# Placing a kernel's matmul operands modulo 256 bytes and gathering its second product's matmuls into one run

## The chip, the cores and the metric

The kernel runs on one core of a Trainium2 chip. The metric is the device time of one execution in microseconds, median of three runs; it was 1442.73 us before the change (1442.69 to 1444.27). The engines are called as the profile calls them: PE (TensorE's matmuls), PEld (its weight loads), DVE (VectorE), ACT (ScalarE), POOL (GpSimd), SP (SyncE).

## What is computed

Three layers in a row, all in float32: a banded attention, a gated feed-forward layer, and a mixture of eight experts whose gate is normalised over rows and columns eight times.

```python
attn_out = _attn_ref(q, k, v, ...)                 # 2 x 8 heads, 768 tokens, 64 wide
x = attn_out.transpose(0, 2, 1, 3).reshape(1536, 512)
h = x @ w_in                                       # 512 -> 2048
x = (h * sigmoid(h)) @ w_out                       # 2048 -> 512
P = exp(x @ w_gate - max)                          # 1536 x 8, then 8 rounds of row and column scaling
for e in range(8):
    h = maximum(x @ w1[e], 0)                      # 512 -> 1024
    out += P[:, e:e+1] * (h @ w2[e])               # 1024 -> 512
```

## The kernel before

**Numbers.** Every matmul operand is a pair of float32r tiles, a high part and the rest (`hi`, `lo`); a product is three matmuls: high by high, high by rest, rest by high. A matmul has a stationary operand, loaded ahead (PEld), and a streamed one.

**Stages.** Tokens go in three blocks of 512 (`TB`), numbered `tb` 0 to 2. Attention fills PE, DVE, ACT and POOL at the start and beside the first blocks of the feed-forward layer ("first layer" below). That layer has 48 steps of 128 hidden columns: 12 matmuls `h` (L237 to L239: stationary `w0`, streamed the tokens `x1`, high and rest) and 12 matmuls `y` (L276: stationary `w1`, streamed `hh`, `hl`). Four steps at the front are done in two halves of 256 tokens, the other 44 have 512 columns. The last block runs without attention beside it.

**Second layer** (`layer2`, from about 421 us). A unit `u` is one half of one expert's hidden columns and one token block: 8 x 2 x 3 = 48 units, `tb` fastest. Its first product, 512 tokens by 512 inputs by 512 hidden columns, is made by a seven-product scheme on 2 x 2 blocks. `x_combine` prepares seven combinations of the tokens in each block (`xc`, with four DVE sums and seven splits), `w_combine` seven combinations of the weights (`wc`, on POOL and ACT). Each of the seven products, numbered 0 to 6, is 12 matmuls of 256 streamed columns at L388 (`h_product`): stationary a slice of `wc[i]`, streamed a block of `xc[i]`. Four PSUM banks collect them: products 0 and 1 in the first (one buffer, tag `h`), 5 and 6 in the second, 4 and 2 in the third, 3 in the fourth (three buffers, tag `a`). DVE adds the banks (`u2` L476, `u3` L480, `h_sum` L410), ACT takes the positive part, DVE the rest (`h_split`, L402 and L403); the four hidden blocks go into five pairs of tiles, the rooms, in turn.

The second product of a unit, `y_part` (L423), is 48 matmuls of 512 streamed columns: four parts `k`, four token tiles `i`, three matmuls each; stationary a slice of a hidden block, streamed a row block of the second weights (`w2c`). `y_add` (L440) weights it by the gate and adds it to the output. It runs one window behind: window `u` computes the seven products of unit `u` and the second product of unit `u - 1`.

**Order in a window** (`window`, L445 to L497) is written by hand: products in `ORDER` 0, 5, 4, 6, 3, 1, 2, and `second()` puts one part of 12 second-product matmuls behind product 5, behind 4, behind 3 and behind 1. `side` is a generator with the rest of the gate (and the third block's `x_combine`); one step of it is taken behind each product. In the last token block of each weight set the next weights are combined product by product (`more`), and in the first block the second weights are split. A scheduler then places the instructions on each engine and moves a few where something would wait.

**Places.** Pools hand out places in a partition one tile behind another, and nearly all tiles are a multiple of 256 bytes long. So all of a pool starts at one byte address modulo 256, set by the odd sizes allocated ahead of it. In the built program these places are:

| operand | role | modulo 256 |
|---|---|---|
| `xc` of blocks 0 and 1 (pool late) | streamed, first product | 96 |
| `xc` of block 2 (pool x) | streamed, first product | 32 |
| `wc` of products 0, 5, 4 (`wc0` to `wc2`, late) | stationary, first product | 96 |
| `wc` of products 6, 3, 1, 2 (`wx0`, `wx1`, ring) | stationary, first product | 32 |
| hidden blocks `room_hh`, `room_hl`, `room_g` | stationary, second product | 32 |
| hidden block `roomh`, `rooml` (late) | stationary, second product | 96 |
| `w2c` (`wx0`, `wx1`, ring) | streamed, second product | 32 |
| first layer, all operands | both | 32 |

While a matmul streams its operand, the stationary operand of the next is loaded. So what stands beside each other in time is the streamed operand of one matmul and the stationary one of the next; by these places they are 0 apart for blocks 0 and 1 in products 0, 5 and 4, and for block 2 in products 6, 3, 1 and 2; streamed 64 above stationary for blocks 0 and 1 in products 6, 3, 1, 2; streamed 64 below (192 above) for block 2 in products 0, 5, 4, and for the second product where a hidden block lies in `roomh`, `rooml`.

Of the kernel before, what the change touches and what calls it, by code (L numbers as in the profile page):

```python
# [8 lines left out]
F32 = mybir.dt.float32  # L9
F32R = mybir.dt.float32r  # L10
# [5 lines left out]
ALU = mybir.AluOpType  # L16
# [4 lines left out]
P = 128  # L21
TB = 512
# [13 lines left out]
WF, RAW = 5, 3  # L36
RING = 4
HB = TB // 2
ORDER = 0, 5, 4, 6, 3, 1, 2
TINY = 1.125 * 2.0**-15  # L40


# [4 lines left out]
class Kernel:  # L47
# [29 lines left out]
    def setup(self, const, pre):  # L77
        nc = self.nc
        n16 = const.tile([P, 2, 4], U16, tag="n16", name="n16")
        for i, src in enumerate((self.n_global, self.n_local)):  # L80
            nc.sync.dma_start(
                n16[:, i, :], src.bitcast(U16).rearrange("(o f) -> o f", o=1).broadcast_to([P, 4])
            )
        self.att_load(0, pre)
        self.att_load(1, const)
        self.ident = const.tile([P, P], F32, tag="ident", name="ident")
        make_identity(nc, self.ident)
        rel, key = self.places(pre)
# [207 lines left out]

    def x_alloc(self, tb):

        if tb < self.NB - 1:
            tiles = [self.gp.tile([P, TB], F32R, tag=f"xc{tb}_{i}", name=f"xc{tb}_{i}") for i in range(14)]
        else:
            tiles = [x[:, c, :] for _ in range(2) for x in self.new_x(f"xc{tb}_{_}") for c in range(self.KD)]
        tiles = [t.rearrange("p (c w) -> p c w", c=2) for t in tiles]
        self.xc[tb] = tiles[:7], tiles[7:14]

    def x_combine(self, tb):
        v, x = self.nc.vector, self.x2[tb]
# [63 lines left out]
    def h_product(self, u, i):  # L373

        nc = self.nc
        ah, al = self.wc[i]
        bh, bl = (x[i] for x in self.xc[u % self.NB])
        name = {0: 0, 1: 0, 5: 1, 6: 1, 4: 2, 2: 2, 3: 3}[i]
        first = i in (0, 5, 4, 3)
        if first:  # L380
            self.hb[name] = self.bank("haaa"[name], f"h2_{u}_{i}")
        ps = self.hb[name]
        n = 0
        for f in range(2):
# [28 lines left out]
    def y_part(self, u, k, tiles=range(4)):  # L413

        nc = self.nc
        f = (2, 3, 0, 1)[k]
        wh, wl = self.w2c[f]
        for i in tiles:
            hh, hl = (x[:, f % 2, i % 2 * P:(i % 2 + 1) * P] for x in self.hq[u][f // 2, i // 2])
            if k == 0:  # L420
                self.y[i] = self.bank("y", f"y2_{u}_{i}")
            for j, (a, b) in enumerate(((hh, wh), (hh, wl), (hl, wh))):
                nc.tensor.matmul(  # L423
                    self.y[i], a, b, start=k == 0 and j == 0, stop=k == 3 and j == 2, skip_group_check=True
                )

    def y_add(self, u, i):

# [16 lines left out]

    def window(self, u, side):

        nc, n_units = self.nc, self.E * self.NH * self.NB
        q, tb = divmod(u, self.NB)
        y = iter(range(4)) if u else iter(())  # L450

        more = tb == self.NB - 1 and q + 1 < self.E * self.NH
        if more:
            self.w_load(q + 1, 1)

        def second():
            k = next(y, None)
            if k is not None:
                self.y_part(u - 1, k)
                if u % self.NB == 0:  # L460
                    self.w_split((2, 3, 0, 1)[k])

        def first(i):
            ps = self.h_product(u, i)
            if more:
                self.w_combine(i)
            next(side, None)
            return ps
# [12 lines left out]
        b4 = first(3)  # L481
        hq[1, 1] = self.h_sum(u3, b3, ALU.add)
        hq[1, 0] = self.h_sum(u3, b4, ALU.subtract)
        second()
        first(1)
        hq[0, 0] = self.h_split(b1)
        second()
        if u:
            if u > self.NB * self.NH:
                for _ in side:  # L490
                    pass
            for i in range(4):
                self.y_add(u - 1, i)
            del self.hq[u - 1]
        first(2)
        hq[0, 1] = self.h_sum(u2, b3, ALU.add)
        if tb == self.NB - 2 and q + 1 < self.E * self.NH:  # L497
            self.w_load(q + 1, 0)

    def layer2(self):  # L500
        n_units = self.E * self.NH * self.NB
        side = self.rest()
        for u in range(n_units):
            self.window(u, side)
        for i in range(4):
            for k in range(4):
                self.y_part(n_units - 1, k, (i,))
            self.y_add(n_units - 1, i)


# [42 lines left out]
    def gate_parts(self):  # L553
# [11 lines left out]
        for it in range(8):  # L565
# [226 lines left out]

    def new_x(self, name):

        return tuple(self.xp.tile([P, self.KD, TB], F32R, tag=t, name=f"{name}{t}", bufs=2) for t in ("xh", "xl"))

    def attention(self, sg):

# [110 lines left out]
    def finish(self):  # L909
# [2 lines left out]
        self.attending = False  # L912
        with tc.tile_pool(name="late", bufs=1, side="right") as self.gp:
            self.gate_load()
            extra = [
                tuple(self.gp.tile([P, TB], F32R, tag=f"wc{i}{t}", name=f"wc{i}{t}") for t in "hl") for i in range(3)
            ]
# [11 lines left out]
            for _ in parts:  # L929
                pass  # L930

            names = [(a, i) for i in range(RING) for a in (0, 1)]
            ws = extra + [
                tuple(self.ring.tile([P, self.DM], F32R, tag=f"w{a}{t}", name=f"wx{a}{t}_{i}") for t in "hl")
                for a, i in names
            ]
# [25 lines left out]
            yield from self.gate_logits(tb)  # L962

    def rest(self):

        yield from self.x_combine(self.NB - 1)
        yield
        yield from self.gate_logits(self.NB - 1)
        yield from self.gate_parts()
# [127 lines left out]
    def arm(self, path):  # L1097
        tc = self.tc
        self.slices, self.raws, self.wfs, self.hs, self.x1, self.x2, self.xc = {}, {}, {}, {}, {}, {}, {}
        with ExitStack() as ctx:  # L1100
# [2 lines left out]
            self.hp = pool(name="hid", bufs=1)  # L1103
            self.wf = pool(name="wf", bufs=WF)
            self.ring = pool(name="ring", bufs=RING)
            self.live = {"wf": 0, 0: 0, 1: 0}
            self.limit, self.stores = SPLIT_START, []
            self.nar, self.freed, self.next_load, self.next_nar, self.next_split = None, [], 0, 0, [0, 0]
# [41 lines left out]
```

## Time and profile before

| | |
|---|---|
| time, median of 3 runs | 1442.73 us (1442.69 to 1444.27) |
| the profiled execution: time, span | 1444.39 us, 1442.6 us |
| mean granted TensorE clock | 0.99 of full |
| PE busy | 1413.3 us, 98%, 8,552 matmuls |
| PEld busy | 1232.1 us, 85% |
| DVE, ACT, POOL busy | 739.9, 487.2, 553.6 us (51, 34, 38%) |
| moved by DMA | 92.18 MB, mean 64 GB/s |

The span is what the profile's records cover; the execution's own time, with what lies around it, is 1.8 us longer. Busy shares are means over stages that differ. A matmul's recorded duration (280 ns for 256 columns, 392 for 512) overlaps that of the next; how fast a run goes is read from the starts of its first and last matmul.

### The profile page before, as it was taken

What the parts mean: (1) busy time and instruction counts of PE and PEld (TensorE: products, weight loads), DVE (VectorE), ACT (ScalarE), POOL (GpSimd) and SP (SyncE); (2) the same over time, 40 slices, a digit from 0 to 9 for tenths busy, and PEclk for the clock granted to TensorE, in tenths of its full rate; (3) what the DMA queues carried; (4) which work ended last, traced back from release to release, by engine and by line L of the source; (5) the groups of instructions that cost most, each with busy time, mean ns of one, the idle gap of its engine ahead of it and who ended that gap; (6) DMA issues with size and microseconds to landing.
All of it is one profiled execution on the core that took longest, in us unless ns stands there. A gap on an engine that the chain in (4) does not pass through costs nothing.

```text
span 1442.6 us, 21250 instructions
## 1 busy us (share of the span) xinstructions
PE 1413.3 (98%) x8552; PEld 1232.1 (85%) x8552; DVE 739.9 (51%) x1298; ACT 487.2 (34%) x949; POOL 553.6 (38%) x489
## 2 busy tenths in 40 slices
PE   8998999999999999999999999999999999999998
PEld 6776687778888989999998999899899899989997
DVE  8899545456353556544354354435444443544443
ACT  6665545555352422222232221223222132322220
POOL 5677755444470423314142331414224141422210
PEclk8899999999999999999999999999999999999999
DMA  9685442222230201011010101102010110201001
GB/s 257 178 245 186 154 121 73 74 74 88 88 103 1 59 1 59 16 44 41 19 50 10 59 16 44 44 16 57 3 59 22 38 45 15 59 0 45 1 28 63
DMA packets 75292, 92.18 MB, mean 64 GB/s; under 512 B 30640, under 2 KB 49072, under 8 KB 75184
## 3 DMA queue, kind: packets, MB, share of 16 engines
q1 hardware_dynamic: 72880, 82.34, 19.2%
q10 hardware_dynamic: 2304, 8.39, 1.5%
q8 instruction: 69, 1.13, 0.3%
q14 instruction: 39, 0.32, 0.1%
HBM read 79.19 MB, written 11.53 MB: 63 GB/s over the span
## 4 chain that ended last, share of the span: by engine, by line
PE 89%; DVE 8%; issue 1%; ACT 1%; POOL 0%; DMA 0%; DVEq 0%; ACTq 0%; SPq 0%; POOLq 0%
PE y L423 37%; PE h L388 32%; PE y L276 7%; PE h L237 3%; PE h L238 3%; PE h L239 3%; PE a_s L726 2%; DVE wf L201 1%; DVE wf L203 1%; DVE wf L199 1%; DVE wf L205 1%; PE a_o L783 1%; PE a_f L764 1%; DVE s L735 1%; DVE st L744 0%
## 5 line engine op out<-in xcount | busy, mean ns | idle before, releaser
L480 DVE TENSOR_TENSOR tabs<-tabs,h 128x512 f32<-128x512 f32 x48 | 33.0, 687 | 333.9 <-PE h L388 333.9
L343 POOL TENSOR_TENSOR wc0l<-wf,wc0h 128x512 fp32r<-128x512 f32 x16 | 21.2, 1323 | 340.3 <-ACT wc0h L342 340.3
L440 DVE SCALAR_TENSOR_TENSOR x<-y,gate,x 128x512 f32<-128x512 f32 x168 | 115.5, 742 | 18.3 <-PE y L423 18.3
L343 POOL TENSOR_TENSOR wx1l<-wf,wx1h 128x512 fp32r<-128x512 f32 x64 | 89.9, 1405 | 79.7 <-ACT wx1h L342 79.5
L402 ACT ACTIVATE room_hh<-tabs 128x512 fp32r<-128x512 f32 x87 | 54.2, 629 | 190.9 <-DVE tabs L410 188.5
L410 DVE TENSOR_TENSOR tabs<-tabs,h 128x512 f32<-128x512 f32 x144 | 98.8, 687 | 19.0 <-PE h L388 16.8
L343 POOL TENSOR_TENSOR wx0l<-wf,wx0h 128x512 fp32r<-128x512 f32 x48 | 62.1, 1293 | 90.3 <-ACT wx0h L342 90.3
L388 PE MATMUL h<-xc,wx1h 128*128 128x256 f32 x512 | 93.4, 280 | 1.7 <-DVE tabs L410 1.7
L388 PE MATMUL h<-xc,wx0h 128*128 128x256 f32 x512 | 93.4, 280 | 0.6 <-DVE tabs L476 0.6
L423 PE MATMUL y<-wx1h,room_hh 128*128 128x512 f32 x232 | 91.2, 393 | 0.0
L423 PE MATMUL y<-wx0h,room_hh 128*128 128x512 f32 x232 | 91.2, 393 | 0.0
L423 PE MATMUL y<-wx0l,room_hh 128*128 128x512 f32 x232 | 90.8, 391 | 0.0
L423 PE MATMUL y<-wx1l,room_hh 128*128 128x512 f32 x232 | 90.8, 391 | 0.0
L423 PE MATMUL y<-wx0h,room_hl 128*128 128x512 f32 x232 | 90.7, 391 | 0.0
L423 PE MATMUL y<-wx1h,room_hl 128*128 128x512 f32 x232 | 90.7, 391 | 0.0
L403 DVE SCALAR_TENSOR_TENSOR room_hl<-tabs,room_hh 128x512 fp32r<-128x512 f32 x87 | 77.6, 898 | 25.5 <-ACT room_hh L402 24.2
L342 ACT ACTIVATE wx1h<-wf 128x512 fp32r<-128x512 f32 x64 | 40.4, 632 | 141.8 <-PE y L423 84.2
L388 PEld LDWEIGHTS h<-xc,wx0h 128*128 128x128 f32 x512 | 82.6, 188 | 5.8 <-DVE tabs L476 0.8
L221 POOL TENSOR_TENSOR w1l<-wf,w1h 128x512 fp32r<-128x512 f32 x48 | 67.0, 1395 | 50.9 <-ACT w1h L220 44.6
L388 PEld LDWEIGHTS h<-xc,wx1h 128*128 128x128 f32 x512 | 80.4, 188 | 4.4 <-DVE tabs L410 1.9
L221 POOL TENSOR_TENSOR w0l<-wf,w0h 128x512 fp32r<-128x512 f32 x48 | 67.0, 1397 | 42.0 <-ACT w0h L220 40.2
L276 PE MATMUL y<-hh,w1h 128*128 128x512 f32 (+1 forms) x208 | 83.0, 399 | 0.0
(270 smaller groups left out, 4143.3 us busy)
## 6 DMA issues: line engine op xcount, KB each, us to landing
wf<-in_moe_w_dram SPq DMA_DIRECT2D x64, 512.0 KB, 3.7
wf<-w SPq DMA_DIRECT2D x32, 512.0 KB, 3.3
ra<-in_moe_w_in_dram SPq DMA_DIRECT2D x16, 512.0 KB, 6.0
rb<-in_moe_w_out_dram SPq DMA_DIRECT2D x16, 512.0 KB, 5.3
w<-wf ACTq DMA_DIRECT2D x16, 512.0 KB, 4.3
vw<-in_v_dram SPq DMA_DIRECT2D x8, 448.0 KB, 4.5
qr<-in_q_dram SPq DMA_DIRECT2D x12, 256.0 KB, 5.8
kr<-in_k_dram SPq DMA_DIRECT2D x12, 256.0 KB, 6.0
```

Of the source, the lines that this page charges most:

```text
L221: nc.gpsimd.tensor_tensor(lo, src, f32(hi), op=ALU.subtract)
L237: nc.tensor.matmul(ps, ah, bh, start=i == 0, stop=False)
L238: nc.tensor.matmul(ps, ah, bl, start=False, stop=False)
L239: nc.tensor.matmul(ps, al, bh, start=False, stop=i == last)
L276: nc.tensor.matmul(self.y[i][:, cols], a, b, start=begin and j == 0, stop=f == self.NF1 - 1 and j == 2, skip_group_check=True,)
L343: self.nc.gpsimd.tensor_tensor(dst[1], src, f32(dst[0]), op=ALU.subtract)
L388: nc.tensor.matmul(ps[:, f * HB:(f + 1) * HB], a[:, k, fs], b[:, k, :], start=first and n == 0, stop=n == 11, skip_group_check=True,)
L402: self.nc.scalar.activation(hi, src, AF.Relu)
L403: self.nc.vector.scalar_tensor_tensor(lo, src, 0.0, f32(hi), op0=ALU.max, op1=ALU.subtract)
L410: self.nc.vector.tensor_tensor(c, a, b, op=op)
L423: nc.tensor.matmul(self.y[i], a, b, start=k == 0 and j == 0, stop=k == 3 and j == 2, skip_group_check=True)
L440: nc.vector.scalar_tensor_tensor(acc, self.y[i], self.gate[:, t, e:e + 1], acc, op0=ALU.mult, op1=ALU.add)
```

## The change

Three things.

*Order.* `ORDER` is 0, 5, 4, 3, 6, 1, 2. In a window the products 0, 5, 4, 3, 6, 1 stand together, then come the four parts of the second product, 48 matmuls, then product 2. Two of the four hidden blocks (the difference with bank four, and the first bank's own split) are made behind the second part, since their rooms are read until then. A step of `side` is taken behind each of the four parts too, none in window 0, and each of the gate's eight rounds has one step more.

*Places.* A pad of 224 bytes in the constants and gaps of 64 and 192 bytes in the pools move every start. The weights `wc` of a product now lie where its place in the order puts them: the first two in the late pool, the next four in one half of the ring, the last in the late pool, and `w2c` in the other half of the ring; the tokens likewise.

| operand | modulo 256 after |
|---|---|
| `xc`, `wc` of products 0, 5, 4, 3, 6, 1 | 0, 64 |
| `xc`, `wc` of product 2 | 64, 0 |
| hidden blocks, all five rooms; `w2c` | 0; 0 |
| first layer: `x1` high; rest in blocks 0, 2; rest in block 1 | 0; 64; 0 |
| first layer: `w0`; `w1`; `hh`, `hl` | 64; 0; 0 |

*Else.* One pad of 96 bytes in the late pool, ahead of the tiles that the rest of the gate takes.

```diff
-ORDER = 0, 5, 4, 6, 3, 1, 2
+ORDER = 0, 5, 4, 3, 6, 1, 2
+PAD_L, PAD_R = 224, 96
+HALF, LINE = 64, 256
...
+        const.tile([P, PAD_L // 4], F32, tag="pad", name="pad")
...
+            tiles = [new(i) for i in range(12)]
+            self.gap(self.gp, HALF)
+            last = [new(i) for i in (12, 13)]
+            self.gap(self.gp, LINE - HALF)
...
         def first(i):
-            ps = self.h_product(u, i)
+            for _ in self.h_product(u, i):
+                pass
             if more:
                 self.w_combine(i)
-            next(side, None)
-            return ps
+            if u:
+                next(side, None)
...
         b2 = first(5)
-        second()
         nc.vector.tensor_tensor(u2, s1, b2, op=ALU.add)
         b3 = first(4)
-        second()
+        b4 = first(3)
         first(6)
         nc.vector.tensor_tensor(u3, s1, b2, op=ALU.add)
-        b4 = first(3)
         hq[1, 1] = self.h_sum(u3, b3, ALU.add)
-        hq[1, 0] = self.h_sum(u3, b4, ALU.subtract)
-        second()
         first(1)
-        hq[0, 0] = self.h_split(b1)
-        second()
-        if u:
+        for k in range(4 if u else 0):
+            for _ in self.y_part(u - 1, k):
+                pass
+            if tb == 0:
+                self.w_split((2, 3, 0, 1)[k])
+            next(side, None)
+            if k == 1:
+                hq[1, 0] = self.h_sum(u3, b4, ALU.subtract)
+                hq[0, 0] = self.h_split(b1)
...
-            yield
-            yield
+            for _ in range(3):
+                yield
...
+        xh = self.xp.tile([P, n], F32R, tag="xh", name=f"{name}xh", bufs=2)
+        if name == "x1_0":
+            self.gap(self.xp, HALF)
+        xl = self.xp.tile([P, n + (LINE - HALF) // 4], F32R, tag="xl", name=f"{name}xl", bufs=2)
...
+            ws = extra[:2] + ws[0] + extra[2:] + ws[1]
```

PE before, window 29, from the end of product 5 over the part that stands behind it; `h_29_5` is the bank of products 5 and 6, `y_28_0` the first tile of unit 28's second product:

```order
L388 MATMUL h_29_5_9276<-xc_1xl,wc1h 128x256
L388 MATMUL h_29_5_9276<-xc_0xl,wc1l 128x256
L423 MATMUL y_28_0_9289<-wx0h_4209,roomh 128x512
L423 MATMUL y_28_0_9289<-wx0l_4210,roomh 128x512
L423 MATMUL y_28_0_9289<-wx0h_4209,rooml 128x512
```

And PE of the change at the same place, where product 4 follows (its weights now in the ring), and then at the end of product 1, where the second product begins:

```order
L407 MATMUL h_29_5_9304<-xc_0xh,wc1h 128x256 x2
L407 MATMUL h_29_5_9304<-xc_0xh,wc1l 128x256
L407 MATMUL h_29_4_9318<-xc_0xl,wx0h_4224 128x256 x2
L407 MATMUL h_29_4_9318<-xc_0xl,wx0l_4225 128x256
```

```order
L407 MATMUL h_29_0_9288<-xc_1xh,wx0h_4230 128x256 x2
L407 MATMUL h_29_0_9288<-xc_1xh,wx0l_4231 128x256
L442 MATMUL y_28_0_9386<-wx1h_4236,roomh 128x512
L442 MATMUL y_28_0_9386<-wx1l_4237,roomh 128x512
L442 MATMUL y_28_0_9386<-wx1h_4236,rooml 128x512
```

The part of 12 that stood behind product 5 has moved behind product 1, where all four parts are now together.

DVE before, window 29, from its first sum to the last addition:

```order
L476 TENSOR_TENSOR tabs<-tabs,h_29_5_9276 128x512
L480 TENSOR_TENSOR tabs<-tabs,h_29_5_9276 128x512
L410 TENSOR_TENSOR tabs<-tabs,h_29_4_9306 128x512
L410 TENSOR_TENSOR tabs<-tabs,h_29_3_9354 128x512
L403 SCALAR_TENSOR_TENSOR room_hl_4218<-tabs,room_hh_4215 128x512
L403 SCALAR_TENSOR_TENSOR room_g_4220<-tabs,room_g_4219 128x512
L440 SCALAR_TENSOR_TENSOR x_1_3491<-y_28_0_9289,gate,x_1_3491 128x512
L403 SCALAR_TENSOR_TENSOR rooml<-h_29_0_9260,roomh 128x512
L440 SCALAR_TENSOR_TENSOR x_1_3491<-y_28_1_9293,gate,x_1_3491 128x512
```

And DVE of the change:

```order
L489 TENSOR_TENSOR tabs<-tabs,h_29_5_9304 128x512
L493 TENSOR_TENSOR tabs<-tabs,h_29_5_9304 128x512
L429 TENSOR_TENSOR tabs<-tabs,h_29_4_9318 128x512
L429 TENSOR_TENSOR tabs<-tabs,h_29_3_9333 128x512
L422 SCALAR_TENSOR_TENSOR room_hl_4245<-tabs,room_hh_4242 128x512
L422 SCALAR_TENSOR_TENSOR rooml<-h_29_0_9288,roomh 128x512
L422 SCALAR_TENSOR_TENSOR room_g_4247<-tabs,room_g_4246 128x512
L460 SCALAR_TENSOR_TENSOR x_1_3516<-y_28_0_9386,gate,x_1_3516 128x512
```

The list is the same but for the first bank's split (`rooml<-h_29_0`), which now stands ahead of all four additions of the second product.

## Rows read from the trace of the kernel before

**Rows 1.** The chain that ended last, by engine (share of the span).

```profile
PE 89%; DVE 8%; issue 1%; ACT 1%; POOL 0%; DMA 0%; DVEq 0%; ACTq 0%; SPq 0%; POOLq 0%
```

**Rows 2.** Waits of PE: line, waited for; us in total, times, longest.

```profile
PE h L237 <- DVE g L257: 10.3, 8, 2.2
...
PE h L388 <- DVE tabs L410: 1.7, 1, 1.7
...
PE h L388 <- DVE room_g L403: 1.0, 1, 1.0
...
PE h L388 <- DVE tabs L476: 0.6, 1, 0.6
```

**Rows 3.** Stretch 607 to 1363: us, busy PE, PEld, DVE, ACT, POOL, clock, DMA.

```profile
607.00:1363.00 756.00, 756.00 (x4756) 682.61 (x4756) 339.76 (x469) 188.10 (x312) 239.19 (x179) 1.00 0.11 33
```

**Rows 4.** Timeline of PE (start us, us, engine, line, operation), window 28, products 0, 5.

```profile
1006.17 0.40 PE L388 MATMUL h<-xc,wc0h 128*128 128x256 f32 x2
...
1009.04 0.40 PE L423 MATMUL y<-wx0h,room_hh 128*128 128x512 f32 x1
```

**Rows 5.** Timeline of PE, window 29, products 6 and 3.

```profile
1036.91 0.28 PE L388 MATMUL h<-xc_0xl,wx0h 128*128 128x256 f32 x1
...
1039.78 0.40 PE L423 MATMUL y<-wx0h,room_hh 128*128 128x512 f32 x1
```

**Rows 6.** Timeline of PE, window 28, products 6 and 3.

```profile
1016.05 0.40 PE L388 MATMUL h<-xc,wx0h 128*128 128x256 f32 x2
...
1018.88 0.39 PE L423 MATMUL y<-wx0h,room_hh 128*128 128x512 f32 x1
```

**Rows 7.** Timeline of PE, window 29, products 0 and 5.

```profile
1027.22 0.28 PE L388 MATMUL h<-xc_0xh,wc0h 128*128 128x256 f32 x1
...
1027.57 0.28 PE L388 MATMUL h<-xc_0xh,wc0h 128*128 128x256 f32 x1
...
1029.95 0.39 PE L423 MATMUL y<-wx0h,roomh 128*128 128x512 f32 x1
```

**Rows 8.** Timeline of PE, window 29, product 4.

```profile
1032.71 0.28 PE L388 MATMUL h<-xc_0xl,wc2h 128*128 128x256 f32 x1
...
1034.13 0.39 PE L423 MATMUL y<-wx1h,roomh 128*128 128x512 f32 x1
```

**Rows 9.** Timeline of PE, window 28, third part of the second product.

```profile
1020.27 0.39 PE L423 MATMUL y<-wx0h,room_hh 128*128 128x512 f32 x1
...
1021.63 0.40 PE L388 MATMUL h<-xc,wx0h 128*128 128x256 f32 x2
```

**Rows 10.** Timeline of PE, windows 28 and 29, six second-product matmuls from roomh.

```profile
1010.43 0.40 PE L423 MATMUL y<-wx0h,roomh 128*128 128x512 f32 x1
...
1011.84 0.40 PE L388 MATMUL h<-xc,wc2h 128*128 128x256 f32 x2
...
1031.34 0.39 PE L423 MATMUL y<-wx0h,room_g 128*128 128x512 f32 x1
```

**Rows 11.** Timeline of PE, window 0.

```profile
420.86 0.40 PE L388 MATMUL h<-xc,wc0h 128*128 128x256 f32 x2
...
426.24 0.28 PE L388 MATMUL h<-xc,wx0l 128*128 128x256 f32 x1
...
429.98 0.28 PE L388 MATMUL h<-xc,wx0l 128*128 128x256 f32 x1
...
433.43 0.40 PE L388 MATMUL h<-xc,wc1h 128*128 128x256 f32 x2
```

**Rows 12.** Timeline of PE, the end of the first layer.

```profile
405.00 0.39 PE L239 MATMUL h<-x_2xh,w0l 128*128 128x512 f32 x1
...
420.64 0.39 PE L276 MATMUL y<-hh,w1l 128*128 128x512 f32 x1
```

**Rows 13.** Timeline of DVE, window 28, the split of the first bank.

```profile
1023.93 0.69 DVE L403 SCALAR_TENSOR_TENSOR room_hl<-h,room_hh 128x512 fp32r<-128x512 f32 x1 [2.71 <-ACT room_hh L402]
```

More of the change, by code (lines that the diff above doesn't have):

```diff
@@ L292, in emit_y, with gap @@
         self.x1.pop(tb)
+    def gap(self, pool, size):
+        self.n_gap += 1
+        pool.tile([P, size // 4], F32, tag=f"gap{self.n_gap}", name=f"gap{self.n_gap}", bufs=1)
     def x_alloc(self, tb):
         if tb < self.NB - 1:
-            tiles = [self.gp.tile([P, TB], F32R, tag=f"xc{tb}_{i}", name=f"xc{tb}_{i}") for i in range(14)]
-        else:
-            tiles = [x[:, c, :] for _ in range(2) for x in self.new_x(f"xc{tb}_{_}") for c in range(self.KD)]
-        tiles = [t.rearrange("p (c w) -> p c w", c=2) for t in tiles]
-        self.xc[tb] = tiles[:7], tiles[7:14]
+            new = lambda i: self.gp.tile([P, TB], F32R, tag=f"xc{tb}_{i}", name=f"xc{tb}_{i}")
+            tiles = [new(i) for i in range(12)]
+            self.gap(self.gp, HALF)
+            last = [new(i) for i in (12, 13)]
+            self.gap(self.gp, LINE - HALF)
+        else:
+            (a, b), (c, last) = (self.new_x(f"xc{tb}_{_}") for _ in range(2))
+            tiles = [x[:, i, :] for x in (a, b, c) for i in range(self.KD)]
+            last = [last[:, i, :] for i in range(2)]
+        hi, lo = ([None] * 7 for _ in range(2))
+        for n, i in enumerate(ORDER):
+            hi[i], lo[i] = (
+                t.rearrange("p (c w) -> p c w", c=2) for t in (last if n == 6 else (tiles[2 * n], tiles[2 * n + 1]))
+            )
+        self.xc[tb] = hi, lo
     def x_combine(self, tb):
@@ L425, in y_part @@
                 )
+                yield
     def y_add(self, u, i):
@@ L446, in window @@
     def window(self, u, side):
-        nc, n_units = self.nc, self.E * self.NH * self.NB
+        nc = self.nc
         q, tb = divmod(u, self.NB)
-        y = iter(range(4)) if u else iter(())
         more = tb == self.NB - 1 and q + 1 < self.E * self.NH
@@ L454, in window @@
             self.w_load(q + 1, 1)
[L456 to L461, printed above, removed]
         def first(i):
-            ps = self.h_product(u, i)
+            for _ in self.h_product(u, i):
+                pass
             if more:
                 self.w_combine(i)
-            next(side, None)
-            return ps
+            if u:
+                next(side, None)
+            return self.hb[{0: 0, 1: 0, 5: 1, 6: 1, 4: 2, 2: 2, 3: 3}[i]]
         s1, u2, u3 = (self.tmp[:, i, :] for i in range(3))
@@ L474, in window @@
         b2 = first(5)
-        second()
         nc.vector.tensor_tensor(u2, s1, b2, op=ALU.add)
         b3 = first(4)
-        second()
+        b4 = first(3)
         first(6)
         nc.vector.tensor_tensor(u3, s1, b2, op=ALU.add)
-        b4 = first(3)
         hq[1, 1] = self.h_sum(u3, b3, ALU.add)
-        hq[1, 0] = self.h_sum(u3, b4, ALU.subtract)
-        second()
         first(1)
-        hq[0, 0] = self.h_split(b1)
-        second()
-        if u:
+        for k in range(4 if u else 0):
[7 more added lines that the diff above has]
+                hq[0, 0] = self.h_split(b1)
+        if u == 0:
+            hq[1, 0] = self.h_sum(u3, b4, ALU.subtract)
+            hq[0, 0] = self.h_split(b1)
+        else:
             if u > self.NB * self.NH:
@@ L506, in layer2 @@
             for k in range(4):
-                self.y_part(n_units - 1, k, (i,))
+                for _ in self.y_part(n_units - 1, k, (i,)):
+                    pass
             self.y_add(n_units - 1, i)
@@ L570, in gate_parts @@
             nc.vector.tensor_tensor(pt, pt, r.unsqueeze(2).to_broadcast([P, nt, e]), op=ALU.mult)
-            yield
-            yield
+            for _ in range(3):
+                yield
             ps = self.bank("a", f"cs_{it}")
@@ L793, in new_x @@
     def new_x(self, name):
-        return tuple(self.xp.tile([P, self.KD, TB], F32R, tag=t, name=f"{name}{t}", bufs=2) for t in ("xh", "xl"))
+        n = self.KD * TB
+        xh = self.xp.tile([P, n], F32R, tag="xh", name=f"{name}xh", bufs=2)
+        if name == "x1_0":
+            self.gap(self.xp, HALF)
+        xl = self.xp.tile([P, n + (LINE - HALF) // 4], F32R, tag="xl", name=f"{name}xl", bufs=2)
+        return tuple(x[:, :n].rearrange("p (c w) -> p c w", w=TB) for x in (xh, xl))
     def attention(self, sg):
@@ L914, in finish @@
             self.gate_load()
-            extra = [
-                tuple(self.gp.tile([P, TB], F32R, tag=f"wc{i}{t}", name=f"wc{i}{t}") for t in "hl") for i in range(3)
-            ]
+            extra = []
+            for i in range(3):
+                if i % 2 == 0:
+                    self.gap(self.gp, LINE - HALF if i else HALF)
+                extra.append(
+                    tuple(self.gp.tile([P, TB], F32R, tag=f"wc{i}{t}", name=f"wc{i}{t}") for t in "hl")
+                )
             room = tuple(self.gp.tile([P, TB], F32R, tag=f"room{t}", name=f"room{t}") for t in "hl")
@@ L930, in finish @@
                 pass
[L932 to L935, printed above, removed]
+            ws = [
+                [tuple(self.ring.tile([P, self.DM], F32R, tag=f"w{a}{t}", name=f"wx{a}{t}_{i}") for t in "hl")
+                 for i in range(RING)]
+                for a in (0, 1)
             ]
+            ws = extra[:2] + ws[0] + extra[2:] + ws[1]
             order = list(ORDER)
@@ L964, in rest @@
     def rest(self):
+        self.gap(self.gp, PAD_R)
         yield from self.x_combine(self.NB - 1)
@@ L1105, in arm @@
             self.ring = pool(name="ring", bufs=RING)
+            self.n_gap = 0
+            self.gap(self.hp, HALF)
+            for a, t in ((0, "h"), (0, "l"), (1, "h"), (1, "l")):
+                if t == "h":
+                    self.gap(self.ring, LINE - HALF if a else HALF)
+                for i in range(RING):
+                    self.ring.tile([P, self.DM], F32R, tag=f"w{a}{t}", name=f"w{a}{t}_room{i}")
             self.live = {"wf": 0, 0: 0, 1: 0}
```

## The prediction

> **What bounds the kernel now.** The reading starts with the chain that ended last: 89% of the span is PE [rows 1], so the time is the time PE needs for its list of matmuls. The table of stretches shows where that holds without exception: from 607 to 1363 us PE is busy for 756.00 of 756.00 us, at a granted clock of 1.00, which is the 2.4 GHz level [rows 3]. The stretch holds 4,756 matmuls; a unit of the second layer has 84 for its seven products (256 columns each) and 48 for the second product of the unit before (512 columns), together 132, so one window takes 756.00 / 4756 x 132 = **20.98 us**. The waits of PE are a few us in all, and in the second layer only three near its start: 1.7, 1.0 and 0.6 us [rows 2]. There is no wait to remove, then; what can change is the distance from one matmul's start to the next. I call it the pitch, and read it from first and last starts in the timeline: twelve matmuls of a product always have the same shape, so a run of 24 divided by 24 needs no model.
>
> The pitch is not one number for one shape. What differs is the byte address, modulo 256, of the operand that a matmul streams, less that of the stationary operand loaded meanwhile for the next one (front part, the table of places). I write that difference as d.
>
> - d = 0, both at 96: 1006.17 to 1009.04 us, 24 matmuls in 2.87 us, **119.6 ns** [rows 4]. Both at 32: 1036.91 to 1039.78, again 2.87 us [rows 5]. So a shift of both operands together by 64 bytes does nothing.
> - d = +64 (streamed at 96, stationary at 32), after a second-product run: 1016.05 to 1018.88, 24 in 2.83 us, **117.9 ns** [rows 6].
> - d = -64 (32 and 96) right after a d = +64 product: 2.73 us for 24; three matmuls of 116.7 ns, then 21 from 1027.57 to 1029.95 in 2.38 us, **113.3 ns** [rows 7].
> - d = -64 after a second-product run: 1032.71 to 1034.13, 12 in 1.42 us, **118.3 ns** [rows 8]; so d = -64 has a fast and a slow rhythm, and the run ahead of it picks one. d = +64 has both too: behind a wait in window 0 it runs 426.24 to 429.98, 33 in 3.74 us, 113.3 ns [rows 11].
> - Second product, d = 0: the first six from 1018.88 to 1020.27, 231.7 ns each; the next six to 1021.63, **226.7 ns** [rows 6, 9]. It settles after about six, and with runs of twelve half of every run is spent settling. At d = -64 six take 1.39 us (231.7 ns) or 1.41 us (235.0 ns) and no run is longer than six, so whether that settles isn't to be seen [rows 7, 10].
>
> **The change part by part.** *Second layer, windows 1 to 47.* Products 0, 5, 4, 3, 6, 1 stand in a row at d = -64 (0 against 64), behind the preceding window's product 2, which is d = +64 (64 against 0): the very switch of rows 7. Their cost: 3 x 116.7 + 69 x 113.3 = 8.17 us. The 48 matmuls of the second product are one run at d = 0: 6 x 231.7 + 42 x 226.7 = 10.91 us. Product 2 follows a second-product run at d = +64: 12 x 117.9 = 1.41 us. Sum 20.49 us against 20.98, so -0.49 us a window, **-22.8 us** over 47. Of that the second product gives about 0.14 us a window, the first products 0.35.
>
> The rule of the Trainium skill that would speak here is in "TensorE: Matmul & The Clock Gate", section "Back-to-back issue gap": a fixed spacing of N / 2.4 + 2.5 ns. By it a window would be an estimated 84 x 109.2 + 48 x 215.8 ns = 19.5 us before and after, and this term zero; the rows, none under 113.3 and 226.7 ns and different for one shape, don't bear it out as a price here.
>
> *Window 0 and the gate's work, windows 0 to 6.* Window 0 takes 12.57 us (420.86 to 433.43) [rows 11]. Its six products now follow layer-one matmuls, as rows 8 follow 512-column ones, so I give them 118 ns as now: nothing gained. The preparation of the third token block (eleven DVE steps) leaves window 0 for window 1, where 48 matmuls stand to cover it. The 3.3 us of waits [rows 2] lay in these two windows behind that DVE work; but window 0's own sums and splits now crowd behind 84 matmuls without cover. Between all gone (-3.3) and half as much again (+1.5) I take -1.5. The eight column-sum matmuls and the last logits interrupt the six-product runs at new places; up to about 200 matmuls may run in the slow rhythm, 200 x 4.6 ns: 0 to +1, taken as +1.
>
> *First layer.* Its weights now stand at 64, its streamed inputs at 0 or 64, its second product at d = 0 as before. Before, all is d = 0 and settled: 405.00 to 420.64 holds 69 matmuls, 226.7 ns each [rows 12]. Now two or three of each three input matmuls are at d = -64 with 512 columns. Lower bound: it settles, 0. Upper bound: 235.0 ns each and every following run settling anew, 12 x 8.3 + 6 x 5.0 = 130 ns a step over 44 full-width steps, +5.7. In the first block PE waits for DVE anyway (10.3 us) [rows 2], and part is covered; I take +2.5.
>
> *Everything else.* The pads, the five-part instead of four-part gate steps and the later place of the third and sixth combination on ACT and POOL add no instruction to PE's list. The splits of two hidden blocks move behind 24 second-product matmuls. Who waits for that: the next window's product 0, for the bank the last split reads. Before, that split starts 1023.93 and lasts 0.69 us, 2.6 us ahead of the need at 1027.22 [rows 7, 13]. After, 24 x 226.7 + 12 x 117.9 ns = 6.9 us remain when the room is free; two ACT and up to three DVE steps of 0.6 to 0.7 us end some 4 us ahead. Cost nothing; without the cover, what it is late by. The DMA issues keep their windows.
>
> Sum: -22.8 - 1.5 + 1 + 2.5 = **-20.8 us**. The profiled execution took 1444.39 us (span 1442.6 and 1.8 around it), which gives 1423.6; the median of the runs shown is 1.66 lower, so I forecast **1422 us**.
>
> **The rivals.**
> - *The slow rhythm stays.* The switch of rows 7 has its operands at 32 and 96, the new one at 0 and 64; or the long run loses its rhythm. Then the six products cost 72 x 118.3 and the window is 8.52 + 10.91 + 1.41 = 20.84: -0.14 x 47 = -6.6, with the other terms 1438. For it: rows 8 and 11 show that the rhythm hangs on what came before. Against: 24 in a row, over a change of product, held it in rows 7, and a common shift of 64 did nothing [rows 4, 5]. A partial lock lies between.
> - *Placement decides nothing*, and the pitch goes with something that the change leaves alone, such as which token block is streamed (the fast rows 7 read the third block, whose inputs lie in another pool). Then the windows keep 20.98 us less at most the settling, and the time stays within 3 us of 1443. This is what the Trainium skill's page "SBUF — State Buffer", section "Who interferes with whom", would make of it: TensorE has two independent read ports and never waits on anyone. Against it: rows 5 and 7 stream the same block, with weights at different places, at 119.6 and 113.3 ns.
> - *Slower: places at 0 modulo 32 are worse than those at 32.* No row of before shows an operand of these lines there. Place: every matmul of the second layer; price: the six products at the d = 0 price of 120 ns and the second product never settling, 235 ns: 8.64 + 11.28 + 1.41 = 21.33 us, +0.35 x 47 = +16, with the first layer 1463. It decides once the three parts pass 20.98 us, so both must fail: 120 ns alone gives 20.96, a draw. Against: the common shift without effect.
> - That the change doesn't do what it says is excluded: the built program has the places and the order given in the front part.
>
> **How the numbers follow.** The forecast gets 0.80, the slow rhythm 0.12, no effect 0.04, slower 0.04. A change of 0.2% (2.9 us) is about what a measurement of this kernel can tell from none: faster 0.92, same 0.04, slower 0.04. The forecast's own ends: early windows -3.3 to +2.5, first layer 0 to +5.7, product 2 in the fast rhythm another -12 x 4.6 ns x 47 = -2.6; together 1414 to 1428, its extremes unlikely at once. The range for 8 in 10 reaches a little into partial locks: **1415 to 1431**.
>
> **What would show it.** Right: a window of 20.5 us in the middle of the second layer; 72 matmuls of a six-product run at 113.3 ns; settled 226.7 ns from about the seventh of 48; product 2 near 118; the last first-layer block a little over 226.7. Wrong: 118 ns through the six products, product runs that differ by token block alone, a PE wait at a window's start, or a first layer that ends over 6 us later.

## The result and the profile after

The change takes the kernel to **1426.12 us** (median of 4 runs, 1425.81 to 1426.89) from 1443.1 (4 runs beside it); ratio 0.9882, 95% interval 0.9865 to 0.9899. That is faster by 1.2%, inside the predicted range and 4 us above the predicted 1422. The profiled execution took 1426.18 us, span 1424.4, against 1444.39 and 1442.6: 18.2 us less.

The chain and PE's waits answer to [rows 1, 2]; the stretch is that of [rows 3].

```profile
PE 89%; DVE 7%; ACT 1%; issue 1%; POOL 1%; DMA 0%; ACTq 0%; DVEq 0%; SPq 0%; POOLq 0%
```

```profile
PE h L407 <- DVE tabs L493: 3.8, 1, 3.8
```

```profile
607.00:1363.00 756.00, 756.00 (x4876) 686.36 (x4875) 341.71 (x479) 195.23 (x320) 236.67 (x180) 1.00 0.11 33
435.00:440.00 5.00, 4.39 (x24) 4.39 (x25) 4.30 (x7) 1.23 (x2) 1.08 (x1) 0.66 0.00 0
435.70:438.70 3.00, 3.00 (x14) 3.00 (x15) 2.97 (x5) 1.23 (x2) 0.38 (x1) 0.50 0.00 0
```

PE is still busy for all of 607 to 1363 us at the same clock, and fits 4,876 matmuls into it where 4,756 were. So the gain is a shorter pitch, no wait. The other two rows show something new: between 435 and 440 us the granted clock is 0.66, and 0.50, the 1.2 GHz level, from 435.70 to 438.70.

The timeline of PE after the change: the start of window 0, the stall at its end, the start of window 7, and one whole window from second-product run to second-product run.

```profile
423.12 0.40 PE L407 MATMUL h<-xc,wc0h 128*128 128x256 f32 x2
...
431.48 0.28 PE L407 MATMUL h<-xc,wx0l 128*128 128x256 f32 x1
435.61 0.80 PE L407 MATMUL h<-xc,wc1h 128*128 128x256 f32 x2 [3.85 <-DVE tabs L493]
...
439.14 0.40 PE L407 MATMUL h<-xc,wc0h 128*128 128x256 f32 x2
...
567.74 0.40 PE L407 MATMUL h<-xc,wc0h 128*128 128x256 f32 x2
...
1006.27 0.40 PE L442 MATMUL y<-wx1h,room_hh 128*128 128x512 f32 x1
...
1007.65 0.39 PE L442 MATMUL y<-wx1h,roomh 128*128 128x512 f32 x1
...
1017.17 0.40 PE L407 MATMUL h<-xc,wc2h 128*128 128x256 f32 x2
...
1018.59 0.40 PE L407 MATMUL h<-xc_0xh,wc0h 128*128 128x256 f32 x2
...
1018.94 0.39 PE L407 MATMUL h<-xc_0xh,wc0h 128*128 128x256 f32 x2
...
1026.76 0.40 PE L442 MATMUL y<-wx1h,roomh 128*128 128x512 f32 x1
```

The window is 1026.76 - 1006.27 = **20.49 us**. Its parts: six second-product matmuls in 1.38 us (230.0 ns each), the other 42 in 9.52 (226.7); product 2 in 1.42 (118.3); three matmuls in 0.35 (116.7), then 69 in 7.82 us (113.3).

Window 7 began at 565.28 us before:

```profile
565.28 0.48 PE L388 MATMUL h<-xc,wc0h 128*128 128x256 f32 x2
```

With window 0's start at 420.86 before [rows 11], the 18.2 us fall into three pieces. Up to window 0: 423.12 - 420.86 = +2.3. Windows 0 to 6: 144.6 against 144.4, +0.2. From window 7 to the end of the span: 1424.4 - 567.74 = 856.7 against 1442.6 - 565.28 = 877.3, -20.7.

### The profile page after: what moved, and what is told of

The parts are those of the page before. It is cut to its first block, busy times and chain, and to the rows that moved or that the text cites. A ratio compares the mean times of both kernels' runs of the same rounds, so it can differ in the third digit from the quotient of the medians.

```text
span 1424.4 us, 21277 instructions
## 1 busy us (share of the span) xinstructions
PE 1395.1 (98%) x8552; PEld 1218.0 (86%) x8552; DVE 731.1 (51%) x1298; ACT 489.9 (34%) x949; POOL 550.9 (39%) x489
## 4 chain that ended last, share of the span: by engine, by line
PE 89%; DVE 7%; ACT 1%; issue 1%; POOL 1%; DMA 0%; ACTq 0%; DVEq 0%; SPq 0%; POOLq 0%
PE y L442 37%; PE h L407 32%; PE y L280 8%; PE h L241 3%; PE h L242 3%; PE h L243 3%; PE a_s L747 2%; DVE wf L205 1%; DVE wf L207 1%; PE a_o L804 1%; PE a_f L785 1%; DVE wf L203 1%; DVE wf L209 1%; PE lg L555 0%; DVE st L765 0%
## 5 line engine op out<-in xcount | busy, mean ns | idle before, releaser
L442 PE MATMUL y<-wx1h,room_hh 128*128 128x512 f32 x464 | 181.0, 390 | 0.0
L442 PE MATMUL y<-wx1l,room_hh 128*128 128x512 f32 x464 | 180.9, 390 | 0.0
L442 PE MATMUL y<-wx1h,room_hl 128*128 128x512 f32 x464 | 180.5, 389 | 0.0
L407 PE MATMUL h<-xc,wx0h 128*128 128x256 f32 x1024 | 176.7, 277 | 0.0
L407 PE MATMUL h<-xc,wx0l 128*128 128x256 f32 x512 | 141.8, 277 | 0.0
L493 DVE TENSOR_TENSOR tabs<-tabs,h 128x512 f32<-128x512 f32 x48 | 33.0, 687 | 149.0 <-PE h L407 148.8
L442 PE MATMUL y<-wx1h,room_g 128*128 128x512 f32 x304 | 106.0, 389 | 0.0
L442 PEld LDWEIGHTS y<-wx1h,room_hl 128*128 128x128 f32 x464 | 87.1, 188 | 18.3
L442 PEld LDWEIGHTS y<-wx1h,room_hh 128*128 128x128 f32 x464 | 87.1, 188 | 17.3
L442 PEld LDWEIGHTS y<-wx1l,room_hh 128*128 128x128 f32 x464 | 87.1, 188 | 16.9
L407 PEld LDWEIGHTS h<-xc,wx0l 128*128 128x128 f32 x512 | 96.1, 188 | 0.0
```

The lines of the kernel that those rows point to most:

```text
L407: nc.tensor.matmul(ps[:, f * HB:(f + 1) * HB], a[:, k, fs], b[:, k, :], start=first and n == 0, stop=n == 11, skip_group_check=True,)
L442: nc.tensor.matmul(self.y[i], a, b, start=k == 0 and j == 0, stop=k == 3 and j == 2, skip_group_check=True)
```

## The experiments

Two questions: what starts the fast rhythm of 113.3 ns, and where the early windows lost what they should have gained. My theory at the outset was the prediction's: places set the rhythm, and a change of sign of d just ahead of a run starts the fast one. Rivals: the order alone, the places alone, a larger distance. Of single executions the window length in the trace decides (from the start of one second-product run to the next; where that is split, from one unit's first product to the next), since single times scatter by several us: the kernel before took 1444.87 us beside runs 1 to 4, 1440.94 beside 5 to 8, and 1440.72 to 1446.06 in nine executions beside run 12. In runs 1 to 6 the time came out up to 4 us away from what was expected with the window that was measured.

| run | window, us | time, us |
|---|---|---|
| 1 order alone | 20.83 mean | 1441.72 |
| 2 places alone | 20.79 | 1437.01 |
| 3 seventh product not reversed | 20.80 | 1438.50 |
| 4 signs mirrored | 20.78 | 1439.49 |
| 5 distance 128 | 20.98 | 1445.76 |
| 6 four reversed, first | 20.80 | 1438.82 |
| 7 third block's preparation on POOL | 20.49 | 1422.27 |
| 8 first layer at d = 0 | 20.49 | 1424.68 |
| 9 both mendings (7 and 8) | 20.49 | 1420.50, median of 5 |
| 10 eight reversed, first | 20.80 | 1438.26 |
| 11 four reversed, last | 20.80 | 1440.36 |
| 12 as 9, none reversed, four at d = 0 | 20.51 | 1421.94, median of 5 |

**1. Order alone.** The new `window` and `ORDER`, without pads, gaps and the new split of the ring (this diff and those below are cut from the diff against the changed kernel):

```diff
...
-        const.tile([P, PAD_L // 4], F32, tag="pad", name="pad")
...
-            ws = extra[:2] + ws[0] + extra[2:] + ws[1]
...
```

> The changed kernel's order (six first products in a row, the 48 matmuls of the second product in one run, the seventh product last) with every tile where it lay before. Theory (the places set the rhythm of the first products, the run length only lets the second product settle): the first products keep 118 to 120 ns, only the 42 settled matmuls of a window's second product gain, a middle window takes 20.8 to 20.9 us (20.49 in the changed kernel, 20.98 before) and the kernel 1436 to 1440 us. Rival (the order is what counts, the places add nothing): windows of 20.5 us and 1424 to 1427 us.

The theory held for the window: 20.83 us. Its trace adds something I had not asked for. This is PE in one window of the second token block, products 0, 5 and 4 at d = 0, then 3, 6 and 1 at d = +64:

```profile
1006.61 0.40 PE L391 MATMUL h<-xc,wc0h 128*128 128x256 f32 x2
...
1010.92 0.39 PE L391 MATMUL h<-xc,wx0h 128*128 128x256 f32 x2
...
1015.00 0.39 PE L426 MATMUL y<-wx0h,room_hh 128*128 128x512 f32 x1
```

36 in 4.31 us are 119.7 ns, as in [rows 4]; the next 36 take 4.08 us, 113.3 ns. So the fast rhythm also began behind a run at d = 0, with no change of sign. I took this up only later (run 12). It did not begin everywhere: in windows 7, 22 and 37, also of the second block, the same 36 stayed slow. Window 22, products 3, 6 and 1, 36 in 4.24 us, 117.8 ns:

```profile
885.93 0.40 PE L391 MATMUL h<-xc,wx0h 128*128 128x256 f32 x2
...
890.17 0.40 PE L426 MATMUL y<-wx0h,room_hh 128*128 128x512 f32 x1
```

**2. Places alone.** `window`, `ORDER` and the side steps of before on the new places:

```diff
-ORDER = 0, 5, 4, 3, 6, 1, 2
+ORDER = 0, 5, 4, 6, 3, 1, 2
...
+            k = next(y, None)
+            if k is not None:
+                for _ in self.y_part(u - 1, k):
+                    pass
...
```

> The changed kernel's places (six products at d = -64, the seventh at +64, second product at 0) with the order of before: four runs of 12 second-product matmuls between the products. Theory (d = -64 is fast only straight behind a d = +64 run, and a second-product run ahead leaves it slow): products 0 and 5 at 113.5 ns, the products behind a second-product run at 118 ns, a middle window 20.81 us, the kernel about 1441 us. Rival (d = -64 is fast by itself): all six at 113.5 ns, a middle window 20.58 us, the kernel about 1430 us.

PE's timeline from product 0 over the first part of the second product and product 4:

```profile
1023.86 0.40 PE L407 MATMUL h<-xc_0xh,wc0h 128*128 128x256 f32 x2
...
1026.59 0.40 PE L442 MATMUL y<-wx1h,roomh 128*128 128x512 f32 x1
...
1029.34 0.40 PE L407 MATMUL h<-xc_0xl,wx0h 128*128 128x256 f32 x2
...
1030.75 0.40 PE L442 MATMUL y<-wx1h,roomh 128*128 128x512 f32 x1
```

Products 0 and 5, straight behind product 2: 24 in 2.73 us, 113.8 ns. Product 4, behind the second product: 12 in 1.41 us, 117.5 ns. Same d, two rhythms; the places alone give 0.19 us a window of the 0.49, the order alone 0.15, and together they give more than the sum.

**3. The seventh product like the others.** Product 2's tokens at 0 and its weights at 64; the gaps move behind the tiles they stood ahead of, and the third block's tiles are read at an offset of 192 bytes:

```diff
-            self.gap(self.gp, HALF)
             last = [new(i) for i in (12, 13)]
+            self.gap(self.gp, HALF)
...
-                if i % 2 == 0:
-                    self.gap(self.gp, LINE - HALF if i else HALF)
+                if i == 0:
+                    self.gap(self.gp, HALF)
...
+            self.gap(self.gp, LINE - HALF)
```

> The changed kernel with the seventh product at d = -64 like the other six, so that no d = +64 run stands ahead of them. Theory (the reversed product is the switch that starts the fast rhythm): all 84 matmuls stay at 118 ns, a middle window takes 84 x 118.0 ns + 10.91 us = 20.82 us, the kernel about 1442 us, as slow as before. Rival (the reversal does nothing; a distance of 64 bytes and a long run are enough): a window of 20.4 to 20.5 us, the kernel 1423 to 1427 us.

```profile
1012.79 0.40 PE L442 MATMUL y<-wx1h,room_hh 128*128 128x512 f32 x1
...
1023.70 0.40 PE L407 MATMUL h<-xc,wc2h 128*128 128x256 f32 x2
...
1025.11 0.40 PE L407 MATMUL h<-xc_0xh,wc0h 128*128 128x256 f32 x2
...
1033.59 0.40 PE L442 MATMUL y<-wx1h,roomh 128*128 128x512 f32 x1
```

PE's timeline, one window: 72 matmuls in 8.48 us, 117.8 ns, and a window of 20.80. Laying one product in seven the other way round is worth 0.31 us a window, most of the gain.

**4. Mirrored.** One constant turns both signs round:

```diff
-HALF, LINE = 64, 256
+HALF, LINE = 192, 256
```

> The changed kernel with both signs turned round by one constant (64 to 192): the six products at d = +64, the seventh at -64. Theory (a change of sign starts the fast rhythm, whichever way round): window 20.49 us, the kernel 1425 to 1428 us. Rival (only the step from +64 to -64 does it, the one that the trace of before shows): six products at 118 ns, window 20.82 us, the kernel about 1442 us.

```profile
1026.27 0.40 PE L407 MATMUL h<-xc_0xh,wc0h 128*128 128x256 f32 x2
...
1034.74 0.40 PE L442 MATMUL y<-wx1h,roomh 128*128 128x512 f32 x1
```

My theory fell: the six products stay at 117.7 ns (72 in 8.47 us), window 20.78. "A change of sign" is not the switch.

**5. Distance 128**, the same line with 128:

> The changed kernel with a distance of 128 bytes in place of 64 (one constant), so that all seven products lie at d = 128 and no sign changes. Theory (what counts is the change of d just ahead of the run): no switch, the products stay slow at 118 to 120 ns, window 20.8 to 21.0 us, the kernel 1441 to 1449 us. Rival (operands far apart within 256 bytes are fast by themselves, and 128 is the farthest): 113.3 ns in all 84, window 20.4 us, the kernel about 1423 us.

```profile
1028.87 0.40 PE L407 MATMUL h<-xc_0xh,wc0h 128*128 128x256 f32 x2
...
1037.51 0.39 PE L442 MATMUL y<-wx1h,roomh 128*128 128x512 f32 x1
```

72 in 8.64 us: 120.0 ns, what d = 0 costs. Apart is not enough; 128 is as bad as none.

**6, 10, 11. Part of the seventh product reversed.** Its weights at 64; the half that is to be reversed streams from 128 (d = +64), the other from 0 (-64), and the twelve are sorted so that the reversed ones come first (four low, or eight high) or last (four low):

```diff
+        todo = [(f, k, a, b) for f in range(2) for k in range(2) for a, b in ((ah, bh), (ah, bl), (al, bh))]
+        if i == 2:
+            todo.sort(key=lambda t: t[3] is not bl)
...
```

> The changed kernel, but in the seventh product only the four matmuls that stream the low half lie at d = +64; they are issued first, and its eight others lie at d = -64 like the six products. Theory (the change from +64 to -64 starts the fast rhythm, and a few matmuls are enough): four at 118 ns, then 80 at 113.4 ns, window 20.45 us, the kernel about 1424.4 us (1426.1 for the changed kernel). Rival (it takes a run of twelve, or a long run to the end of the product): 118 ns all the way, window 20.82 us, the kernel about 1442 us.

> As the run with four reversed matmuls (where the fast rhythm never started), but with eight: in the seventh product those that stream the high half lie at d = +64 and are issued first, then the four others at d = -64. Theory A (the number of reversed matmuls decides, and eight are enough): 8 at 118 ns, then 76 at 113.4 ns, window 20.47 us, the kernel about 1425 us. Theory B (the reversed run must reach the end of the product, or hold high and low halves in turn): 118 ns all the way, window 20.80 us, the kernel about 1438 us.

> As the run with four reversed matmuls, but the four come last in the seventh product, straight ahead of the next window's six, behind eight at d = -64. Theory A (the number of reversed matmuls decides, four are too few wherever they stand): window 20.80 us, the kernel about 1438 us. Theory B (the change of sign must fall between two products): the six products run at 113.4 ns, window 20.49 us, the kernel about 1426 us.

All three stay slow, a middle window takes 20.80 us. Here is PE with eight reversed, from product 2 over product 0 to the second product:

```profile
1023.46 0.28 PE L409 MATMUL h<-xc,wc2h 128*128 128x256 f32 x1
...
1024.87 0.40 PE L409 MATMUL h<-xc_0xh,wc0h 128*128 128x256 f32 x2
...
1033.35 0.40 PE L444 MATMUL y<-wx1h,roomh 128*128 128x512 f32 x1
```

72 in 8.48 us, 117.8 ns. Number and position of the reversed matmuls decide nothing here. What the three lack and run 1 had is a matmul at d = 0 ahead of the run. In the changed kernel the last matmul of product 2 streams from 64 while product 0's weights, also at 64, are loaded: d = 0, once a window ahead of the six products. With both halves' places split as here no matmul ahead of them has that.

**12. No reversal, d = 0 instead.** As run 9 (below), product 2's weights at 64, its high half at 0 and its low half at 64, the low half's matmul third of three:

```diff
...
+                for a, b in ((ah, bh), (al, bh), (ah, bl)) if i == 2 else ((ah, bh), (ah, bl), (al, bh)):
...
```

> The kernel with both mendings (1420.5 us), but in the seventh product no matmul is reversed: eight lie at d = -64, and the four that stream the low half, each third one and the last of the twelve, at d = 0. In every run so far that became fast without a hiccup, a 256-column matmul at d = 0 stood just ahead of the fast run, and in the three that split the seventh product with d = +64 and -64 there was none. Theory A (such a matmul at d = 0, followed by a distance of 64, starts the fast rhythm): the six products at 113.4 ns, part of the seventh too, window 20.45 to 20.55 us, the kernel 1418.5 to 1423 us. Theory B (it takes the d = +64 run ahead of it as well): 118 ns and more, window 20.80 to 20.84 us, the kernel 1434 to 1437 us.

```profile
1009.85 0.28 PE L408 MATMUL h<-xc,wc2h 128*128 128x256 f32 x1
...
1011.26 0.40 PE L408 MATMUL h<-xc_0xh,wc0h 128*128 128x256 f32 x2
...
1012.65 0.39 PE L408 MATMUL h<-xc_0xh,wc1h 128*128 128x256 f32 x2
...
1019.45 0.40 PE L443 MATMUL y<-wx1h,roomh 128*128 128x512 f32 x1
```

Product 2 takes 1.41 us as ever; product 0 1.39, its first matmuls still slow; products 5 to 1 60 matmuls in 6.80 us, **113.3 ns**. Theory A holds for the six products: no d = +64 is needed, 256-column matmuls at d = 0 ahead are enough in this kernel. Its other half does not hold: product 2 stays slow, though three such matmuls stand inside it, each followed by two at d = -64. The ratio to before is 0.9856 (0.9832 to 0.9881), not told apart from run 9.

**7. The third block's preparation on POOL.**

```diff
-        v, x = self.nc.vector, self.x2[tb]
+        v, x = self.nc.gpsimd if tb == self.NB - 1 else self.nc.vector, self.x2[tb]
```

> The changed kernel with the eleven preparation steps of the third token block on POOL in place of DVE. Theory (pulled ahead into window 0, they hold the sums that free PE's bank, which costs 3.8 us of waiting and about 1.5 us at the half clock behind it): the wait at window 1's start falls below 1 us, the clock stays up, the kernel 1420.5 to 1423 us. Rival (the wait is made by window 0's own sums, crowded behind 84 matmuls): the wait stays over 3 us and the kernel within 1425 to 1428 us.

DVE of the changed kernel in window 0: preparation (L336, L341), then the sum L493, for whose bank PE waits.

```profile
422.79 0.69 DVE L336 TENSOR_TENSOR kT<-x 128x512 f32<-128x512 f32 x1
...
426.23 0.68 DVE L336 TENSOR_TENSOR kT<-qr,x 128x512 f32<-128x512 f32 x1
...
431.54 1.75 DVE L341 TENSOR_TENSOR xc_1xh<-x,xc_1xh 128x512 fp32r<-128x512 f32 x1
...
434.88 0.68 DVE L493 TENSOR_TENSOR tabs<-tabs,h 128x512 f32<-128x512 f32 x1
```

And POOL beside the step at 431.54:

```profile
431.09 1.65 POOL L374 TENSOR_TENSOR kT<-wf,wf 128x512 f32<-128x512 f32 x1 [0.63 <-DVE xc_0xl L341]
```

With the preparation on POOL, DVE reaches L493 at 430.43 us, and PE at the same place reads:

```profile
431.52 0.28 PE L407 MATMUL h<-xc,wx0l 128*128 128x256 f32 x1
431.64 0.40 PE L407 MATMUL h<-xc,wc1h 128*128 128x256 f32 x2
...
433.41 0.40 PE L407 MATMUL h<-xc,wc0h 128*128 128x256 f32 x2
```

No wait at this place, and the row of the stretches that read 0.66 reads 1.00:

```profile
435.00:440.00 5.00, 3.80 (x34) 3.60 (x32) 4.28 (x4) 1.24 (x2) 5.00 (x4) 1.00 0.00 2
```

In the changed kernel 16 matmuls stand behind the wait, four of window 1's product 5 and window 0's product 2; they take 439.14 - 435.61 = 3.53 us, nearly all at the 1.2 GHz level. Here 14 stand at this place, two and twelve, and take 433.41 - 431.64 = 1.77 us. Sixteen at 118 ns would take 1.89 us, so the half clock cost an estimated 1.6 us on top of the 3.85 us of waiting. A wait of 1.2 us for L489, which the changed kernel does not have, comes up later in window 1; windows 0 to 6 take 140.3 us, 4.3 less, and the time is 1422.27 us.

**8. First layer at d = 0.** All of `x1` at 64, beside `w0`; `xc` of the third block reads the same tiles at an offset:

```diff
...
+        off = off or ((16, 16) if name == "x1_1" else (0, 0))
+        pair = []
+        for t in ("xh", "xl"):
+            if name == "x1_0":
+                self.gap(self.xp, HALF if t == "xh" else LINE // 2)
+            pair.append(self.xp.tile([P, n + (LINE - HALF) // 4], F32R, tag=t, name=f"{name}{t}", bufs=2))
...
```

> The changed kernel with the first layer's streamed inputs at 64 like its weights, so that its input matmuls lie at d = 0 as before; the second layer's places unchanged. Theory (the layer-one loss of 2.2 us comes from the input matmuls at d = -64, 235 to 238 ns in the last block against 226.7): layer one ends at 420.9 us instead of 423.1 and its last block is back at 226 to 227 ns; the kernel about 1424 us. Rival (the loss comes from elsewhere, such as preparation at the start): layer one ends at 423 us and the kernel stays at 1426 us.

The last block of layer one, the stretch 380 to 420 us, before, after and in this run:

```profile
380.00:420.00 40.00, 40.00 (x178) 33.11 (x178) 12.02 (x15) 18.68 (x33) 29.00 (x22) 1.00 0.29 91
```

```profile
380.00:420.00 40.00, 40.00 (x175) 32.36 (x174) 11.89 (x15) 17.91 (x31) 28.59 (x22) 1.00 0.33 105
```

```profile
380.00:420.00 40.00, 40.00 (x177) 32.85 (x176) 11.64 (x15) 19.07 (x33) 29.40 (x22) 1.00 0.34 111
```

178, 175 and 177 matmuls in 40 us. By first and last starts the layer's last 69 take 226.7 ns each before [rows 12], some 230 after and 228 here, so the 226 to 227 expected was only half reached. Window 0 starts at 421.04 us: 2.1 of the 2.3 us are back. A single start scatters, too: run 1, whose first layer lies as before, starts window 0 at 422.37 us. Still, the seven traces with the changed kernel's first layer lie at 422.66 to 424.51 us and the three with this one (runs 8, 9 and 12) at 419.69 to 421.10, so the loss and its cause stand.

**9. Both mendings.**

> The changed kernel with both mendings together: the third block's preparation on POOL (3.9 us by itself) and the first layer's inputs at 64 (1.5 us by itself, 2.1 us by the end of layer one). Theory (the two are at different places of the path and add up): 1426.1 - 3.9 - 1.5 to 2.1 = 1420.1 to 1420.7 us, faster than the changed kernel and than before. Rival (layer one's earlier end lets window 0 wait for work that comes no earlier): about 1422 us.

1420.50 us (1420.11 to 1421.91), ratio 0.9836 (0.9823 to 0.9850), an interval wholly under the changed kernel's. The two add up, and this version beats both.

## Why the prediction was right, and where it was off

- *The middle windows:* 20.49 us forecast, 20.49 measured, and each part of the sum as priced: 113.3 ns, 118, 226.7 from the seventh of 48 on. From window 7 on the sum said 41 x -0.49 = -20.1; measured -20.7.
- *Why they are fast* was half right, and the price came out by luck. That the rhythm hangs on what came before held (runs 2 and 3). But "the very switch of rows 7" was read as a change of d from +64 to -64; runs 6, 10 and 11 make that change without effect, and run 12 does without it. What stands ahead of the six products in every middle window that became fast at d = -64, and in none of runs 3, 6, 10 and 11, is a 256-column matmul at d = 0. Rows 7 held it too, unnoticed, and so the price was right. A full cause it is not: run 4 has that matmul and stays slow, and the last section shows more such places.
- *The first layer:* +2.5 forecast, +2.3 measured, and by run 8 made where I put it.
- *The early windows* are the step that failed, by 3.6 us: windows 1 to 6 at -0.49 each, -1.5 and +1 made -3.4, measured +0.2. The miss lies in windows 0 to 2, which were to give -2.5 and lost 1.1 (window 3 starts at 479.62 us before and 482.94 after); windows 3 to 6 gave -0.9 where -1.0 was priced. The step was "The preparation of the third token block (eleven DVE steps) leaves window 0 for window 1". It did not: all eleven ran from 422.79 us on, in window 0 and ahead of L493, and the wait was 3.85 us where I left 1.8. On top came the half clock, an estimated 1.6 us, which I had not counted. Part of the wait is that DVE's steps stretch beside POOL: 0.68 us alone at 426.23 us, 1.75 at 431.54, where POOL works from 431.09 on; the trace of before has such a step too, 1.78 us at 426.98. On that the Trainium skill, "SBUF — State Buffer", section "Who interferes with whom", says that a DVE instruction with two SBUF inputs contends with a GpSimd instruction that reads SBUF; the trace agrees. Run 7 takes the preparation away from DVE, and all of it comes back: windows 0 to 6 take 4.1 us less than before.
- *The allowance for the median:* I took 1.66 us off because the profiled execution before stood that far above its median. After, it stands on it (1426.18 and 1426.12). That is the rest of the 4.1 us between 1422 and 1426.
- *The rivals:* "the slow rhythm stays" is what runs 3 and 4 are, 20.80 and 20.78 us against its 20.84; so it was a near thing, since these two differ from the changed kernel in places alone. "Placement decides nothing" falls with runs 3 and 5, one kernel with three places: 20.49, 20.80, 20.98 us. The third, that places at 0 modulo 32 are worse than those at 32, did not show.

## What to carry to other kernels

Where PE is never idle, read the pitch of each run of matmuls from first and last starts, and beside it the places modulo 256 of the streamed operand and of the next stationary one; at 256 columns that was worth 113.3 to 120 ns for one shape here. Check what the run ahead leaves behind as well as the run itself. And when a reorder takes matmuls away from beside an engine's queue, look at what a scheduler may pull into the gap: the wait that was to go came back longer, and the clock fell behind it.

## What was not expected of the hardware

- One shape, three pitches: 120.0 ns at d = 0 and 128, 117.8 or 113.3 at +64 and -64, the last two chosen by what ran just before. Second-product matmuls, at 512 columns, left the slow one behind them in every middle window, though most of them are at d = 0 themselves.
- Fast began behind a 256-column matmul at d = 0 (after, runs 1 and 12), but not always. In run 4 the same matmul stands at the same spot, between -64 and +64, and nothing happened; in three windows of run 1 the products behind d = 0 stayed slow. In the changed kernel itself the six products of window 4 stayed slow behind that matmul. There two column-sum matmuls stand ahead of product 2, and product 2 had itself run fast at d = +64: nine matmuls in 1.02 us, 113.3 ns, then 60 of the six products in 7.07 us, 117.8 ns. What decides between the two rhythms is open.

```profile
503.31 0.39 PE L407 MATMUL h<-xc,wc2h 128*128 128x256 f32 x2
...
504.33 0.40 PE L407 MATMUL h<-xc,wc0h 128*128 128x256 f32 x2
...
511.40 0.40 PE L407 MATMUL h<-xc,wx0h 128*128 128x256 f32 x2
```

- Interruptions can start it too. Run 3 has no such matmul ahead of its six products, but in its gate windows, behind two column-sum matmuls, PE went on at 0.34 us for three, 113.3 ns each:

```profile
482.67 0.36 PE L595 MATMUL cs<-gate,ones 128*128 128x96 f32 x2
...
483.25 0.39 PE L407 MATMUL h<-xc,wc0h 128*128 128x256 f32 x2
...
483.59 0.39 PE L407 MATMUL h<-xc,wc0h 128*128 128x256 f32 x2
```

- After one wait of 3.85 us PE ran 16 matmuls (435.61 to 439.14 us) at or near the 1.2 GHz level before the clock came back.
